# A constant row by selector matmuls, a first batch loaded by head group and a padded odd key chunk in a one-core attention and adapter-mixture kernel

## The chip, the cores and the metric

The kernel runs on one core of a Trainium2 chip. The metric is the device time of one execution, in microseconds (us), and smaller is better. A profile's span is some 1.7 us shorter than the time of the same execution (300.2 and 301.93 for the kernel before), so spans are compared with spans here and times with times.

Engines are named as in the profile: PE is TensorE's matmul, PEld its weight load, DVE is VectorE, ACT is ScalarE, POOL is GpSimd, SP is the engine that issues most of the DMAs. SPq is SP's time in issuing them.

On one core the "slow" state is only a label for runs over 1.5% above the fastest of the same kernel; ratios use the other runs, which the tables call fast. The one profile of the kernel before carries the slow label itself (301.93 us, clock 0.893), though it is only 0.5% above the fastest timed run of its call.

## The reference

Attention over 8 batches, 12 heads, 448 keys and 64 numbers per head, then a mixture of eight small adapters (rank 16), two of them chosen for each row:

```python
def _attn_ref(q, k, v):
    scores = np.matmul(q, k.transpose(0, 1, 3, 2)) / np.sqrt(64)
    attn = softmax(scores)                      # cut: the usual max, exp, sum
    return np.matmul(attn, v)                   # (8, 12, 448, 64)

def _moe_ref(x, w_gate, A, B):                  # x: (3584, 768)
    logits = x @ w_gate                         # 8 experts, the best two are kept
    # ... cut: w = softmax over the two
    delta = sum over the two of  w * ((x @ A[e]) @ B[e])
    return x + delta
```

## The kernel before

The kernel writes the attention output as a constant row plus a small rest. The constant row is the mean of v over the keys, one row of 768 numbers for a whole batch. The rest comes from exp(score) - 1 and from v less its mean, both in fp16. TensorE makes the means and keeps each as two fp16 halves, high and low, in a small tile `mhl` (called `s["m"]` in the code). For the adapters the constant row is multiplied once per batch by the weights (`cz`). That matmul contracts over the 768 numbers, so it needs the row turned upright: tile `mT`, with 128 partitions and six columns of chunks.

A list scheduler written in Python fixes, before anything runs, the order of the instructions on each engine. TensorE executes that order strictly: an instruction that waits stops all those behind it (from 90 to 103 us of the profile before, while one matmul waits, TensorE starts no other).

The constant row before (a scatter by eight DMAs, then a DMA transpose):

```python
def const_row(b):
    yM, mT = Buf(p_yM, "yM"), Buf(p_mT, "mT")
    for g in range(4):
        for j in range(2):
            P.op("SP", lambda e, g=g, h0=h0, j=j: [e.dma_start(        # L504
                V(yM)[32 * j:32 * j + 2, :]..., V(s["m"])[32 * g:32 * g + 2, :]...)],
                r=[s["m"], b_init], w=[part], holds=[yM], cost=0.06, dma=0.05, ...)
    P.op("SP", lambda e: [e.dma_start_transpose(V(mT)[:, :, 0:48], V(yM)[0:48, :])],   # L508
         r=parts + [yM, b_init], w=[mT], cost=0.06, dma=0.5, ...)
    def fc(e):
        for c in range(6):                                             # L515
            x = e.matmul(ps[:, V(tc), 0:144], V(mT)[:, c, :], W16[:, c, :], ...)
    # ... cut: two small vector instructions put the result into cz
```

The score tiles: each batch has 21 of them, each with one exp on ScalarE ("an exp" below is this instruction, 168 in all). They go in pairs through a ring of two PSUM slots of two banks each. `holds` of the first tile of a pair names both slots (the code is condensed):

```python
p_sc = Pool([(0, 1), (2, 3)])
...
prev = P.op("PE", fs, r=[g["qT"], g["kT"]], w=g["slot"],
            holds=[x for y in two[i:] for x in y["slot"]], ...)       # L473, L467
P.op("ACT", ... e.activation(E32, ps[slot], AF.Exp, scale=SC) ..., cost=0.80, tag="exp")   # L483
P.op("POOL", ... E16 = E32 * 1.0 - 1.0 ...)
```

The start of the program (condensed), which fixes what comes early:

```python
load_qk(0); load_v(0, q0[:2])
weights(v0)                      # w_gate, six pieces of A (L306), B
load_qk(1, v0); load_v(1, q0[-1:] + v0)
for b in range(NB):
    if b == 0:
        transposes(0, 0); transposes(0, 1); means(0); transposes(0, 2)
    for u in range(NU):          # three head groups of a batch
        attention(b, u, ...)
        if u == 0: const_row(b)
        if b + 1 < NB: transposes(b + 1, u)
    if b + 1 < NB: means(b + 1)
    if b >= 1: moe(b - 1)
```

The softmax here doesn't subtract the row's maximum and nothing guards it: scores larger than these inputs give would overflow.

Of the kernel before, what the change touches and what calls it, by code (L numbers as in the profile page):

```python
# [6 lines left out]
ALU = mybir.AluOpType  # L7
# [8 lines left out]
MO = 6.0  # L16
TO = -3.0
SO = -3.0
BI = 0.0
# [29 lines left out]
class Prog:  # L49
# [38 lines left out]
    def schedule(self, window=400):  # L88
# [4 lines left out]
        dmaq = {e: 0.0 for e in ENG}  # L93
        left = len(self.ops)
        LAT = 0.08

        def ready(o):
            t = 0.0
            e_pe = o.eng == "PE"
            for d in o.deps:  # L100
                if d.end is None:
                    return None
                t = max(t, d.end + (0 if d.eng == o.eng and d.dma is None and (e_pe or d not in o.raw) else LAT))
# [4 lines left out]
            for bs in need.values():  # L108
# [4 lines left out]
                for s in range(p.n):  # L113
                    ten = p.tenant[s]
                    if ten is None:
                        av.append(0.0)
                    elif ten.left == 0:
                        av.append(max(x.end for x in ten.ops) + LAT)
# [6 lines left out]
        while left:  # L125
# [43 lines left out]
            if o.dma is not None:  # L169
                free[e] = st + o.cost  # L170
                dmaq[e] = max(dmaq[e], st + o.cost) + o.dma
                o.end = dmaq[e] + 1.8
# [14 lines left out]
def bass_mha_softmax__then__mixture_of_adapters_kernel(  # L187
# [9 lines left out]
    with contextlib.ExitStack() as ctx:  # L197
# [15 lines left out]
        p_kT = pool("kT", 4, [128, 2, NS], F16)  # L213
# [7 lines left out]
        p_yM = pool("yM", 1, [48, ND], F16)  # L221
        p_mT = pool("mT", 1, [128, 6, 128], F16)
# [10 lines left out]
        sel2 = sb("sel2", [128, 128], F16)  # L233
        cS = sb("cS", [128, 3, 32])
# [13 lines left out]
        b_init = fixed("init")  # L248
# [12 lines left out]
        def setup_dve(e):  # L261
# [9 lines left out]
            for x in p_yM.views:  # L271
                i = e.memset(x[:, :], 0.0)
            for x in p_mT.views:
                i = e.memset(x[:, :, :], 0.0)
# [3 lines left out]
        def setup_dve2(e):  # L278
# [8 lines left out]
            for x in p_w16.views:  # L287
                xv = x.rearrange("p (h two) d -> p h two d", two=2)
                e.memset(xv[0:64, :, 0, 64:65], 1.0)
                i = e.memset(xv[64:128, :, 1, 64:65], 1.0)  # L290
# [8 lines left out]


        def weights(gate=()):
            P.op("SP", lambda e: [e.dma_start(wg32[:, :, :], moe_w_gate.rearrange("(c p) e -> p c e", p=128))],
                 w=[b_wg], cost=0.06, dma=1.0, prio=0.5, after=gate)
            bs = [fixed("A%d" % c) for c in range(6)]
            for c in range(6):
# [3 lines left out]
                    w=[bs[c]], cost=0.06, dma=1.2, prio=0.5, after=gate)  # L309
            P.op("SP", lambda e: [e.dma_start(B32[:, :], moe_B.rearrange("e r d -> (e r) d"))],  # L310
                 w=[b_B32], cost=0.06, dma=1.0, prio=0.5, after=gate)
# [10 lines left out]
        def load_qk(b, gate=()):  # L322
            s = st[b]
            pr = 6.0 * b - 9
            s["q"], s["k"] = Buf(p_q16, "q"), Buf(p_k16, "k")
            s["qp"] = {}
            groups = [(0, 2), (2, 6)] if b == 0 else [(0, 6)]
            for (h0, h1) in groups:
                for nm, src in (("q", q), ("k", k)):
                    for half in range(2):  # L330
                        part = fixed("ld")
                        for hs in range(h0, h1):
                            s["qp"][(nm, hs, half)] = part

                        def f(e, h0=h0, h1=h1, nm=nm, src=src, half=half):
                            dst = s[nm].pool.views[s[nm].slot]
                            return [e.dma_start(
                                dst[64 * half:64 * half + 64, h0:h1, :, :].rearrange("p h c d -> p h (c d)"),
                                src[b, 6 * half + h0:6 * half + h1, :, :].rearrange("h (p c) d -> p h (c d)", c=7))]
                        P.op("POOL", f, w=[part], holds=[s[nm]], cost=0.68, dma=0.32 * (h1 - h0), prio=pr, tag="ld", after=gate)  # L340

        def load_v(b, gate=()):
            s = st[b]
            pr = 6.0 * b - 8
            s["v"], s["w"] = Buf(p_v32, "v"), Buf(p_w32, "w")
            s["vp"] = []
            vv = v[b].rearrange("h (p c) d -> p h c d", c=7)
            for half in range(2):
                part = fixed("ldv")
                s["vp"].append(part)  # L350
                P.op("SP", lambda e, half=half: [e.dma_start(  # L351
                    s["v"].pool.views[s["v"].slot][64 * half:64 * half + 64, :, :, :].rearrange("p h c d -> p h (c d)"),
                    vv[:, :, 3 * half:3 * half + 3, :].rearrange("p h c d -> p h (c d)"))],
                    w=[part], holds=[s["v"]], cost=0.06, dma=2.0, prio=pr, after=gate, tag="ldv")
            for half in range(2):
                part = fixed("ldw")
                s["vp"].append(part)
                P.op("SP", lambda e, half=half: [e.dma_start(  # L358
                    s["w"].pool.views[s["w"].slot][64 * half:64 * half + 64, :, :],
                    v[b].rearrange("(h two) (p c) d -> two p h c d", c=7, two=2)[half, :, :, 6, :])],  # L360
                    w=[part], holds=[s["w"]], cost=0.06, dma=0.6, prio=pr, after=gate, tag="ldw")
# [4 lines left out]
        def transposes(b, u):  # L366
            s = st[b]
            pr = 6.0 * b + 2 * u + TO
            for nm, pl in (("q", p_qT), ("k", p_kT)):
# [4 lines left out]
                parts = [s["qp"][(nm, 2 * u, hf)] for hf in range(2)]  # L374
                order = list(range(7)) if nm == "q" else [0, 3, 1, 4, 2, 5, 6]
# [7 lines left out]
                P.op("PE", f, r=[src, b_id] + parts, w=[tb], holds=[dst], cost=0.42, prio=pr, mode="t", tag="tr", nsig=2)  # L383

                def ev(e, tb=tb, dst=dst, nm=nm):
                    bk = ps[:, V(tb), :].bitcast(F16)[:, 0:896].rearrange("p (c g x) -> p g c x", c=7, g=2)
# [303 lines left out]
        for b in range(NB):  # L690
# [8 lines left out]
            for u in range(NU):  # L699
                attention(b, u, last=(b == NB - 1 and u == NU - 1))  # L700
                if u == 0:
                    const_row(b)
# [154 lines left out]
```

## Time and profile before

| | kernel before |
|---|---|
| time, median of 3 | 300.35 us |
| span of the profile | 300.2 us |
| TensorE busy, idle | 217.4 us, 82.8 us (300.2 less 217.4) |
| exp number 21 ends (batch 0) | 52.6 us |
| exp number 42 ends (batch 1) | 109.3 us |
| exp number 168 ends (batch 7) | 269.9 us |

The ends of exps are read from ScalarE's timeline. They cut the span into stage 1 (batches 0 and 1), stage 2 (batches 2 to 7) and a tail (the last expert work).

From the first part of the page of the kernel before: busy time, share of the span and count of instructions.

```profile
span 300.2 us, 8596 instructions
PE 217.4 (72%) x3624; PEld 141.1 (47%) x3624; DVE 165.0 (55%) x461; ACT 169.4 (56%) x205; POOL 178.1 (59%) x211
```

No engine is full. The stretches view of the same kernel has for each stretch its length, then each engine's busy time with its count, then the granted TensorE clock, the DMA share and GB/s. These are the three stages:

```profile
0.00:109.30 109.30, 59.19 (x884) 36.60 (x885) 37.16 (x107) 46.78 (x54) 53.79 (x72) 0.78 0.87 144
109.30:269.90 160.60, 139.16 (x2514) 92.17 (x2510) 109.59 (x302) 120.62 (x148) 122.77 (x139) 0.98 0.78 133
269.90:300.20 30.30, 19.06 (x239) 12.38 (x235) 18.20 (x54) 2.01 (x5) 1.55 (x2) 0.84 0.42 112
```

Stage 1 takes 109.3 us for two batches, TensorE idles 50.1 us of it, and the clock is only 0.78. Stage 2 takes 160.6 us for six. The list of waits says what stage 1 waits for (waiter, releaser: us in total, times, longest):

```profile
PE ps L515 <- DMA mT<-yM: 26.7, 3, 13.6
ACT E_5 L483 <- PE ps L473: 26.1, 13, 7.5
ACT E_2 L483 <- PE ps L473: 22.2, 10, 14.4
```

The constant-row matmul waits 26.7 us, in three waits, for the transposed row. ScalarE's longest waits, 7.5 and 14.4 us, are the same stalls seen one engine further on. SP's timeline shows the path of that row (start, length, what):

```profile
18.84 11.08 SPq L306 DMA_DIRECT2D A<-in_moe_A_dram  x6
...
39.44 5.52 SPq L504 DMA_DIRECT2D yM<-mhl  x8
...
49.64 2.39 SPq L508 DMA_TRANSPOSE mT<-yM  x1
59.48 5.41 SPq L504 DMA_DIRECT2D yM<-mhl  x8
68.28 1.20 SPq L508 DMA_TRANSPOSE mT<-yM  x1
...
80.63 5.59 SPq L504 DMA_DIRECT2D yM<-mhl  x8
...
89.67 3.20 SPq L508 DMA_TRANSPOSE mT<-yM  x1
```

Eight issues cost SP about 5.5 us per batch, and the transpose can only be issued after them. The chain that ended last (start, length, what) shows how long its data then took to land:

```profile
49.64 9.76 DMA mT<-yM
...
68.28 2.43 DMA mT<-yM
...
89.67 13.44 DMA mT<-yM
```

All three lie on the critical chain, and they span 9.8, 2.4 and 13.4 us.

### The profile page before, as it was taken

How to read it: one execution, taken by the hardware profiler on the slowest of the kernel's cores; microseconds unless marked ns; L12 is line 12 of the kernel's file. 1: busy time of each engine (PE TensorE's matmuls, PEld its weight loads, DVE VectorE, ACT ScalarE, POOL GpSimd, SP SyncE). 2: the span in 40 equal slices, each digit the busy share in tenths (PEclk: the TensorE clock that was granted, in tenths of full speed). 3: DMA queues.
4: the chain of work that ended last, by engine and by line, in shares of the span. 5: the costliest groups of instructions: out<-in, count | busy, mean ns of one | idle time of the engine just before them, and what ended most of it. 6: DMA issues, size and time to landing. Idle time of an engine off the chain costs nothing.

```text
span 300.2 us, 8596 instructions
## 1 busy us (share of the span) xinstructions
PE 217.4 (72%) x3624; PEld 141.1 (47%) x3624; DVE 165.0 (55%) x461; ACT 169.4 (56%) x205; POOL 178.1 (59%) x211
## 2 busy tenths in 40 slices
PE   1757666075880286899979898898689988996863
PEld 0434434033560154466546655565356655765441
DVE  6116524040830136866677668666284787686664
ACT  1526385141780077787878786986269777870100
POOL 8258466241673068777989986797267867771000
PEclk9967959665996599999999999999699999999887
DMA  6979999836929703596994999299947233853326
GB/s 78 222 112 179 189 229 212 143 48 125 176 69 210 102 4 48 115 272 99 164 173 87 242 123 211 68 244 137 140 130 149 56 88 63 110 133 82 99 84 183
DMA packets 68966, 40.54 MB, mean 135 GB/s; under 512 B 40640, under 2 KB 65216, under 8 KB 68928
## 3 DMA queue, kind: packets, MB, share of 16 engines
q1 hardware_dynamic: 56064, 28.99, 50.7%
q0 software_dynamic: 12864, 11.01, 26.2%
q8 instruction: 28, 0.46, 0.7%
q14 instruction: 10, 0.08, 0.1%
HBM read 33.84 MB, written 11.01 MB: 149 GB/s over the span
## 4 chain that ended last, share of the span: by engine, by line
PE 35%; DMA 15%; SPq 14%; ACT 13%; DVE 12%; issue 6%; POOL 4%; DVEq 0%; POOLq 0%; ACTq 0%
DMA mT<-yM 9%; PE ps L548 8%; PE ps L473 6%; SPq L504 5%; DMA v_0<-in_v_dram 4%; PE ps L660 4%; SPq L306 4%; SPq L358 4%; PE ps L407 3%; PE ps L664 3%; ACT E_1 L483 2%; PE ps L550 2%; ACT E_0 L483 2%; SPq L351 2%; PE ps L467 2%
## 5 line engine op out<-in xcount | busy, mean ns | idle before, releaser
L473 PE MATMUL ps<-qT,kT 64*128 64x448 f16 x288 | 45.3, 378 | 15.3 <-ACT E_1 L483 5.5
L483 ACT ACTIVATE E_5<-ps 128x896 f32<-128x896 f32 x28 | 25.7, 918 | 26.1 <-PE ps L473 26.1
L483 ACT ACTIVATE E_2<-ps 128x896 f32<-128x896 f32 x28 | 25.8, 922 | 22.3 <-PE ps L473 22.2
L388 ACT COPY kT<-ps 128x896 f16<-128x896 f16 x24 | 21.9, 912 | 16.6 <-PE ps L380 16.6
L483 ACT ACTIVATE E_4<-ps 128x896 f32<-128x896 f32 x28 | 25.7, 918 | 9.8 <-PE ps L473 9.7
L483 ACT ACTIVATE E_1<-ps 128x896 f32<-128x896 f32 x28 | 25.7, 917 | 8.6 <-PE ps L473 8.5
L483 ACT ACTIVATE E_0<-ps 128x896 f32<-128x896 f32 x28 | 25.7, 916 | 8.1 <-PE ps L473 8.1
L483 ACT ACTIVATE E_3<-ps 128x896 f32<-128x896 f32 x28 | 25.8, 921 | 5.8 <-PE ps L473 5.8
L660 PE MATMUL ps<-B,zT 128*128 128x384 f16 x64 | 22.6, 353 | 4.7 <-DVE qT L388 1.4
L515 PE MATMUL ps<-W,mT 128*128 128x144 f16 x48 | 5.4, 261 | 27.2 <-DMA mT<-yM 26.7
L556 DVE TENSOR_SCALAR den<-ps 128x8 f32<-128x8 f32 x48 | 7.9, 165 | 30.5 <-PE ps L550 30.3
L388 DVE COPY qT<-ps 128x896 f16<-128x896 f16 x24 | 14.9, 620 | 17.0 <-PE ps L380 16.8
L473 PEld LDWEIGHTS ps<-qT,kT 64*128 64x128 f16 x288 | 9.5, 95 | 29.0 <-issue 6.6
L664 PE MATMUL ps<-mhl,sel 128*128 128x192 f16 x128 | 22.5, 261 | 0.0
L518 DVE CAST cz<-ps 64x144 f16<-64x144 f32 x8 | 2.4, 298 | 28.5 <-PE ps L515 28.5
L515 PEld LDWEIGHTS ps<-W,mT 128*128 128x128 f16 x48 | 3.8, 111 | 28.7 <-issue 14.3
L417 DVE CAST mhl<-ps 128x192 f16<-128x192 f32 x8 | 2.9, 357 | 23.6 <-PE ps L411 23.6
L664 PEld LDWEIGHTS ps<-mhl,sel 128*128 128x128 f16 x128 | 13.2, 103 | 4.9 <-issue 1.2
L467 PE MATMUL ps<-qT,kT 64*64 64x448 f16 x96 | 15.4, 404 | 0.0
L635 PE MATMUL ps<-W,yT 128*128 128x128 f16 x192 | 14.2, 219 | 0.0
L660 PEld LDWEIGHTS ps<-B,zT 128*128 128x128 f16 x64 | 6.3, 98 | 16.7 <-issue 2.2
L486 POOL TENSOR_SCALAR E_6<-E_3 128x896 f16<-128x896 f32 x5 | 4.7, 937 | 15.0 <-ACT E_3 L483 15.0
(276 smaller groups left out, 852.3 us busy)
## 6 DMA issues: line engine op xcount, KB each, us to landing
v_0<-in_v_dram SPq DMA_DIRECT2D x8, 576.0 KB
v_1<-in_v_dram SPq DMA_DIRECT2D x8, 576.0 KB
q_1<-in_q_dram POOLq DMA_DIRECT2D x8, 336.0 KB, 6.4
k_1<-in_k_dram POOLq DMA_DIRECT2D x8, 336.0 KB, 8.3
out_dram<-o_0 SPq DMA_DIRECT2D x13, 192.0 KB
out_dram<-o_1 SPq DMA_DIRECT2D x12, 192.0 KB, 3.0
out_dram<-o_4 SPq DMA_DIRECT2D x11, 192.0 KB, 3.3
q_0<-in_q_dram POOLq DMA_DIRECT2D x6, 336.0 KB, 9.1
```

Of the source, the lines that this page charges most:

```text
L306: P.op("SP", lambda e, c=c: [e.dma_start(A32[:, c, :].rearrange("p (e r) -> p e r", e=NE), moe_A[:, 128 * c:128 * c + 128, :].rearrange("e ...
L358: P.op("SP", lambda e, half=half: [e.dma_start(s["w"].pool.views[s["w"].slot][64 * half:64 * half + 64, :, :], v[b].rearrange("(h two) (p ...
L388: return [e.tensor_copy(o, bk) if nm == "q" else e.copy(o, bk)]
L467: r.append(e.matmul(ps[sl, bk, 0:NS], V(kT)[sl, pi, 384:448], V(qT)[sl, pi, :], start=True, stop=True, tile_position=(64 * h, 64 * h)))
L473: r.append(e.matmul(ps[:, bk, 0:NS], V(kT)[sl, pi, 128 * t:128 * t + 128], V(qT)[sl, pi, :], start=True, stop=True, tile_position=(64 * h, ...
L483: P.op("ACT", lambda e, g=g, e32=e32: [e.activation(V(e32)[:, :, :], ps[:, V(g["slot"][0])[0]:V(g["slot"][0])[0] + 2, 0:NS], AF.Exp, scale ...
L504: P.op("SP", lambda e, g=g, h0=h0, j=j: [e.dma_start(V(yM)[32 * j:32 * j + 2, :].rearrange("p (h x) -> p h x", h=12)[:, h0:h0 + 5:2, :], V ...
L515: x = e.matmul(ps[:, V(tc), 0:144], V(mT)[:, c, :], W16[:, c, :], start=(c == 0), stop=(c == 5))
L548: e.matmul(o, V(gs[c])[:, hi, c0:c0 + 128], V(s["v16"])[:, h, c, :], start=(c == 0), stop=False)
L635: e.matmul(o, V(yT[t])[:, c, :], W16[:, c, 0:128], start=(c == 0), stop=False)
L660: e.matmul(ps[:, V(to), 0:384], V(zT)[:, t, :], B16[:, 384 * hh:384 * hh + 384], start=True, stop=True, skip_group_check=True)
L664: x = e.matmul(ov[:, par, :, :], sel[:, 2 * par + hh, :], V(m)[:, :], start=False, stop=True, skip_group_check=True)
```

## The change

Its intent is to take the constant row off the DMA queue, to let the first batch start on a third of its data, and to give the odd key chunk (keys 384 to 447 of two head pairs) the same matmul form as the full chunks. The scheduler's costs and priorities were retuned at the same time. The core of the diff, with cuts:

```diff
-TO = -3.0
-SO = -3.0
+TO = -2.5
+SO = -1
-        LAT = 0.08
+        LAT = {"PE": 0.2, "ACT": 0.18, "DVE": 0.12, "POOL": 0.12, "SP": 0.1}
-        dmaq = {e: 0.0 for e in ENG}
+        dmaq = 0.0
...                                            (and many cost= and dma= figures)
-            for g in range(4):                            # constant row: 8 DMAs
-                for j in range(2):
-                    P.op("SP", ... e.dma_start(V(yM)[32 * j:32 * j + 2, :]..., V(s["m"])[32 * g:...]))
-            P.op("SP", lambda e: [e.dma_start_transpose(V(mT)[:, :, 0:48], V(yM)[0:48, :])], ...)
+            def fm(e):                                    # 6 selector matmuls
+                for par in range(2):
+                    for j in range(3):
+                        i = e.matmul(ps[64 * par:64 * par + 64, V(tm), 68 * j:68 * j + 68],
+                                     V(s["m"])[:, 64 * j:64 * j + 64], selT[:, par, :, :]...,
+                                     start=True, stop=True, tile_position=(0, 64 * par))
+            P.op("PE", fm, ...)
+            P.op("DVE", ... e.tensor_copy(V(mT)..., ps[:, V(tm), 0:204]...) ...)
...
-                order = list(range(7)) if nm == "q" else [0, 3, 1, 4, 2, 5, 6]
+                order = list(range(7)) if nm == "q" else [6, 0, 3, 1, 4, 2, 5, 6]
...                                            (odd chunk: 128 wide, two matmuls into one bank)
-                                    r.append(e.matmul(ps[sl, bk, 0:NS], V(kT)[sl, pi, 384:448], V(qT)[sl, pi, :],
-                                                      start=True, stop=True, tile_position=(64 * h, 64 * h)))
+                                    kc = V(kT)[sl, 896:1024] if pi == 0 else V(kT)[sl, 0:128]
+                                    r.append(e.matmul(ps[:, bk, 0:NS], kc, V(qT)[sl, pi, :], start=(pi == 0), stop=(pi == 1),
+                                                      tile_position=(64 * h, 0)))
...
-        load_qk(0)
-        load_v(0, q0[:2])
-        weights(v0)
-        load_qk(1, v0)
-        load_v(1, q0[-1:] + v0)
+        for u in range(NU):
+            load_qk(0, (u,))
+        load_v(0, (0,), q0[:2])
+        load_v(0, (1, 2), q0[:2])
+        load_qk(1, gate=v0)
+        load_v(1, gate=v0)
+        weights(v0)
...
-                transposes(0, 1)
-                means(0)
-                transposes(0, 2)
+                means(0, (0,))
             for u in range(NU):
                 attention(b, u, last=(b == NB - 1 and u == NU - 1))
+                if b == 0 and u < 2:
+                    transposes(0, u + 1)
+                    if u == 0:
+                        means(0, (1, 2))
                 if b + 1 < NB:
                     transposes(b + 1, u)
```

## The prediction

> **What bounds it now.** Busy table: TensorE 217.4 of 300.2 us (72%), no other engine above 59%. The stretches view splits the span: 104.5 to 271.5 us is a steady part with TensorE 145 of 167 us busy at clock 0.97, bounded by TensorE plus short score-exp round trips; 271.5 to 300 is a serial tail (last expert stage); 0 to 104.5 holds only two of the eight batches and is bounded by waits. TensorE executes in order, and the list of waits names them: constant-row matmul <- DMA mT, 26.7 us in 3 waits, the longest 13.6. They lie at 54-60, 66-71 and 90-103 us. The SP timeline shows why: eight scatter issues of 0.62 to 0.7 us each per batch (64 = 42 us of queue in all), then a DMA transpose which lands after 2.4, 9.8 and 13.4 us because bulk loads are in flight. The clock there is 0.60 to 0.63. Also: 3.2 us until v of batch 0 lands (18.8), 5 us at 35-40 for ScalarE's cast of B (its DMA sits behind 11 us of A issues), and 3.8 us at 209 without a releaser.
>
> **Removed.** The scatter, the transpose, and with them all 26.7 us of wait, and most half-clock restarts (estimate 5 us, from those clocks). v of batch 1 is issued ahead of the weights (was 30.6 us, now about 18.5), so the 5 us ScalarE wait should go.
>
> **Added.** Six small matmuls and one vector copy per batch (estimate 0.3 and 0.35 us, from similar ones here); 48 more transposes, 0.036 us each from 0.5 us per 14: 1.7 us; two more vector subtractions per batch, vector being 67% busy in the steady part: nothing. The odd chunk keeps four 448-column matmuls (0.50 us a group, full chunks 0.48): nothing.
>
> **Moved.** The built order of TensorE puts q transposes and means of batch 1 before the third head group of batch 0. So after 14 exps (about 30 us) I expect TensorE to wait for v of batch 1. At the measured 172 GB/s (2.75 MB landed by 18.4 us) that lands at 34-36: a new wait of 4 to 8 us. Loading by head group itself gains 1 to 3 us: batch 1's loads still wait for batch 0's v. From about 38 us 28 exps at 1.2 us (the undisturbed pace at 76-89 us) put the end of batch 1's exps near 72 us, against 109. The y transposes now come amid loads, so the first expert stage may wait 0 to 5 us.
>
> **Sum.** 300.4 - 37 (first two batches) - 4 (order, part of the 3.8) = 259 us. 80%: 249 to 272. Faster by over 2%: 0.97; within 2%: 0.02; slower: 0.01.
>
> **Signs.** Right: no wait of the constant-row matmul above 1 us; exp number 42 ends at 66-80 us; the stretch from it to the last exp stays 155-168 us and the tail 27-30; mean clock rises from 0.89 to 0.93 or more; a wait of TensorE for v of batch 1 near 30-36 us. Wrong: a new multi-microsecond wait for yT, W or later loads in 50-110 us.
>
> **What could make it wrong.** The loads: 40.5 MB pass in 259 us at 156 GB/s, while the busiest stretches reached about 200; if loads fall behind, the steady pace slows (time up to 275). Or the steady part was itself limited by late buffers and gains from the retuned scheduler costs (down to 248). The Trainium skill ("TensorE: Matmul & The Clock Gate", What's actually happening) says idle windows of about 3.4 us halve the clock; this trace agrees (0.60 at 89.7-104.5), so every wait removed or added counts for more than its length.

## More of the kernel before

The time scatters more than usual for this kernel. The kernel before took 300.3 to 300.89 us on the first chip and 287 to 305 us in the five later calls.

Where few runs are fast, their mean is the mean of the luckiest, so the text also looks at the median of all.

## The result, and the profile after

The changed kernel took 275.56 us, the median of 4 runs (274.39 to 277.66), beside 300.5 us (300.3 to 300.89) for the kernel before. Its results are correct. The ratio is 0.9176, with a 95% interval of 0.9118 to 0.9234. (A ratio here is the mean time of one kernel's fast runs over that of the other's of the same rounds, so it is not quite the ratio of the medians.) It is faster, as predicted, but 16.6 us slower than the 259 us predicted and outside the range of 249 to 272.

| us | before | after | difference |
|---|---|---|---|
| span | 300.2 | 272.7 | -27.5 |
| TensorE busy | 217.4 | 212.2 | -5.2 |
| TensorE idle | 82.8 | 60.5 | -22.3 |
| exp 14 ends | 39.9 | 28.6 | -11.3 |
| exp 21 ends | 52.6 | 53.5 | +0.9 |
| exp 42 ends | 109.3 | 80.8 | -28.5 |
| exp 42 to exp 168 | 160.6 | 160.8 | +0.2 |
| tail | 30.3 | 31.1 | +0.8 |

The first part of the page of the changed kernel:

```profile
span 272.7 us, 8828 instructions
PE 212.2 (78%) x3756; PEld 142.1 (52%) x3756; DVE 170.1 (62%) x502; ACT 169.0 (62%) x205; POOL 180.4 (66%) x215
```

The stretches view of the changed kernel, with the same three stages and columns as before:

```profile
0.00:80.80 80.80, 52.31 (x883) 33.53 (x883) 37.54 (x127) 45.42 (x54) 54.21 (x74) 0.92 1.01 162
80.80:241.60 160.80, 141.53 (x2645) 96.65 (x2642) 113.73 (x321) 121.63 (x149) 125.08 (x141) 0.98 0.80 145
241.60:272.70 31.10, 18.37 (x241) 11.87 (x237) 18.88 (x55) 1.99 (x5) 1.14 (x2) 0.92 0.43 114
```

All of the gain lies in stage 1, and within it in batch 1: exps 22 to 42 took 27.3 us instead of 56.7. The clock of stage 1 rose from 0.78 to 0.92. Stage 2 did not move. The changed kernel's list of waits:

```profile
ACT E L515 <- PE ps L505: 50.8, 66, 1.9
...
ACT kT L403 <- PE ps L393: 18.3, 5, 9.8
```

The waits for the constant row's DMA are gone. ScalarE still waits 50.8 us in all for scores, but in 66 short waits, none above 1.9 us. A new wait of 9.8 us stands in the second line. Where it lies, ScalarE's timeline of the changed kernel shows (idle time before a piece and its releaser are in brackets):

```profile
26.83 1.73 ACT L515 ACTIVATE E<-ps 128x896 f32<-128x896 f32 x2 [0.49 <-PE ps L505]
38.36 2.57 ACT L403 COPY kT<-ps 128x896 f16<-128x896 f16 x3 [9.81 <-PE ps L393]
...
51.90 0.83 ACT L316 CAST W<-A 128x768 f16<-128x768 f32 x1 [4.39 <-DMA A<-in_moe_A_dram]
```

ScalarE finishes the 14th exp at 28.6 us and has nothing to do until 38.4. TensorE's timeline for those microseconds, same kernel:

```profile
31.05 1.58 PE L393 MATMUL ps<-ident,q 128*64 128x128 f16 x28
33.67 0.58 PE L393 MATMUL ps<-ident,q 128*64 128x128 f16 x14
35.17 1.18 PE L430 MATMUL ps<-v,cS 128*32 128x192 f32 x24 [0.92 <-DMA vr<-in_v_dram]
...
37.66 1.17 PE L393 MATMUL ps<-ident,k 128*64 128x128 f16 x32 [0.47 <-DVE mhl L441]
```

TensorE transposes q of batch 1 and makes the means of batch 1's v (L430), and only then transposes the k that the third head group of batch 0 needs. It waits for data only 0.92 us of that. The reason is in the code: the buffers for the transposed q and k are handed out strictly in the order in which the program creates them, and the changed start creates those of batch 1's first group before those of batch 0's third.

The second new wait, 4.39 us for A at 47.5 to 51.9 us, comes from SP's timeline of the changed kernel. The same six issues took 11.08 us before:

```profile
22.68 23.08 SPq L310 DMA_DIRECT2D A<-in_moe_A_dram  x6
```

They now run beside the loads of batch 1. As a result the constant-row matmul of batch 0 meets a wait after all, though not for its own data; from the list of TensorE's waits in that stretch:

```profile
PE ps L550 <- DVE W L320: 3.2, 1, 3.2
```

### The profile page after: what moved, and what is told of

It reads as the page before. It is cut to its first block, busy times and chain, and to the rows that moved or that the text cites. A ratio compares the mean times of both kernels' runs of the same rounds, so it can differ in the third digit from the quotient of the medians.

```text
span 272.7 us, 8828 instructions
## 1 busy us (share of the span) xinstructions
PE 212.2 (78%) x3756; PEld 142.1 (52%) x3756; DVE 170.1 (62%) x502; ACT 169.0 (62%) x205; POOL 180.4 (66%) x215
## 3 DMA queue, kind: packets, MB, share of 16 engines
q0 software_dynamic: 12928, 11.01, 27.3%
## 4 chain that ended last, share of the span: by engine, by line
PE 44%; DVE 19%; SPq 10%; DMA 8%; ACT 8%; POOL 6%; issue 3%; DVEq 0%; POOLq 0%
PE ps L583 12%; PE ps L505 8%; SPq L310 6%; ACT E L515 6%; DVE v L469 6%; POOL E L518 4%; DMA A<-in_moe_A_dram 4%; PE ps L695 4%; PE ps L393 3%; PE ps L585 3%; PE ps L430 3%; DVE o L703 3%; PE ps L670 3%; DVE y L599 3%; DVE vr L460 3%
## 5 line engine op out<-in xcount | busy, mean ns | idle before, releaser
L518 POOL TENSOR_SCALAR E<-E 128x896 f16<-128x896 f32 x168 | 154.2, 940 | 53.0 <-ACT E L515 50.5
L515 ACT ACTIVATE E<-ps 128x896 f32<-128x896 f32 x168 | 145.4, 918 | 51.0 <-PE ps L505 50.8
L583 PE MATMUL ps<-v,E 128*128 128x65 f16 x1152 | 59.3, 199 | 8.5 <-POOL E L518 3.6
L583 PEld LDWEIGHTS ps<-v,E 128*128 128x128 f16 x1152 | 52.8, 100 | 19.3 <-DVE y L599 4.7
L585 PE MATMUL ps<-vr,E 128*128 128x65 f16 x384 | 54.8, 196 | 0.0
L703 DVE SCALAR_TENSOR_TENSOR o<-y,ps 128x384 f32<-128x384 f16 x64 | 34.6, 550 | 10.2 <-PE ps L699 8.3
L585 PEld LDWEIGHTS ps<-vr,E 128*128 128x128 f16 x384 | 38.7, 101 | 0.0
L599 DVE TENSOR_TENSOR y<-ps,den 128x512 f16<-128x512 f32 x48 | 33.1, 689 | 1.0
L403 ACT COPY kT<-ps 128x896 f16<-128x896 f16 x24 | 21.8, 914 | 18.3 <-PE ps L393 18.3
L469 DVE TENSOR_TENSOR v<-v,ps 128x576 f16<-128x576 f32 (+1 forms) x32 | 22.1, 727 | 0.3
L699 PE MATMUL ps<-mhl,sel 128*128 128x192 f16 x128 | 21.8, 254 | 0.0
L393 PE MATMUL ps<-ident,k 128*64 128x128 f16 x384 | 16.2, 233 | 5.0 <-DVE v L469 2.4
L393 PEld LDWEIGHTS ps<-ident,q 128*64 128x64 f16 x336 | 11.3, 119 | 14.7 <-DMA q<-in_q_dram 6.9
```

What stands on the lines that cost most here:

```text
L393: x = [e.transpose(bk[64 * h:64 * h + 64, 128 * i:128 * i + 128], V(src)[:, 2 * u + h, c, :], ident[:, :]) for h in range(2)]
L403: return [e.tensor_copy(o, bk) if nm == "q" else e.copy(o, bk)]
L469: return [e.tensor_tensor(v16[:, f, h, :, :], v32[:, f, h, :, :], mb[:, f, :, None, :].broadcast_to([128, nu, 3, DH]), ALU.subtract)]
L515: P.op("ACT", lambda e, g=g, e32=e32: [e.activation(V(e32)[:, :, :], ps[:, V(g["slot"][0])[0]:V(g["slot"][0])[0] + 2, 0:NS], AF.Exp, scale ...
L518: P.op("POOL", lambda e, g=g, e32=e32: [e.tensor_scalar(V(g["e16"])[:, :, :], V(e32)[:, :, :], 1.0, -1.0, ALU.mult, ALU.add)], r=halves + ...
L583: e.matmul(o, V(gs[c])[:, hi, c0:c0 + 128], V(s["v16"])[:, h, c, :], start=(c == 0), stop=False)
```

## The experiments

Eighteen kernels ran, in five calls, each call on one chip. Two theories stand at the start. Theory one: stage 1 fell short of the prediction because of named, mendable waits there (the order of batch 0's third group; the A loads), and mending them brings the missing time back. Its rival: those waits are in the shadow of something else, and the missing time went elsewhere, into stage 2 or into the nature of the steady part.

| kernel | chip's call | median, us (range) | fast mean, us (runs) | ratio to before |
|---|---|---|---|---|
| constant row alone | 1 | 271.54 (268.67-273.52) | 270.58 (3 of 4) | 0.9204 |
| third group first | 1 | 269.29 (268.32-270.70) | 269.40 (4 of 4) | 0.9164 |
| A in long rows | 1 | 272.14 (270.00-273.91) | 272.05 (4 of 4) | 0.9277 |
| old priorities | 1 | 275.68 (273.56-276.31) | 275.31 (4 of 4) | 0.9365 |
| the change | 2 | 272.09 (270.27-277.17) | 271.82 (5 of 6) | - |
| third first + cost of A | 2 | 275.74 (271.71-280.22) | 273.17 (3 of 6) | - |
| old scheduler | 2 | 280.62 (273.35-282.35) | 274.78 (2 of 6) | - |
| old odd chunk | 2 | 273.30 (271.75-276.33) | 272.83 (5 of 6) | - |
| the change | 3 | 275.07 (270.34-277.48) | 271.07 (2 of 6) | 0.9231 |
| third first + weights early | 3 | 270.22 (268.02-274.99) | 269.75 (5 of 6) | 0.9186 |
| constant row alone, again | 3 | 268.61 (266.80-270.44) | 268.65 (6 of 6) | 0.9161 |
| third first + old odd chunk | 3 | 272.51 (267.09-278.81) | 268.38 (2 of 6) | 0.9139 |
| the change | 4 | 275.83 (274.94-280.15) | 275.84 (5 of 6) | - |
| + TensorE work | 4 | 277.78 (274.66-279.19) | 276.57 (4 of 6) | - |
| + VectorE work | 4 | 275.73 (274.06-278.93) | 275.38 (5 of 6) | - |
| constant row, weight casts later | 4 | 268.93 (267.36-270.31) | 269.02 (6 of 6) | - |
| constant row + own slot only | 5 | 257.53 (255.47-259.07) | 257.34 (6 of 6) | 0.8806 |
| the change + own slot only | 5 | 272.48 (265.49-274.70) | 265.61 (2 of 6) | 0.9101 |

In the calls without a ratio, the kernel before had too few fast runs for one. For calls 3 and 5, where 4 and 3 of its 11 runs were fast, the record gives the ratios but leaves each verdict "unclear"; for call 1 it says "faster". Where a stage is quoted below it comes from the one profile of that kernel.

### 1. The constant row alone

The kernel before with nothing but the constant row's hunk (which also gives `mT` two buffers in place of one and narrows it; these were not separated), once in call 1 and once more, unaltered, beside the change in call 3.

```diff
 (kernel before)
-            yM, mT = Buf(p_yM, "yM"), Buf(p_mT, "mT")        # 8 DMAs + DMA transpose
+            tm, mT = Buf(p_t, "tm"), Buf(p_mT, "mT")         # 6 matmuls + 1 copy
             ... (as in the change, nothing else)
```

> The kernel before with the constant row alone changed (selector matmuls and a vector copy for the 8 scatters and the DMA transpose); loads, odd chunk and scheduler constants as before. If the constant row is nearly all of the gain: the holes at 53-60, 66-72 and 90-103 us close, exp 42 ends at 78 to 85 us, time 268 to 278. If the head-group loading, odd chunk and retuned constants carry a good part: time 283 to 292, with exp 42 after 90 us.

> The constant row alone in the kernel before, again, now beside the control. If it carries the whole gain: ratio to the control 0.99 to 1.01. If loads, odd chunk and retuning add to it: 1.015 or more; if they cost: 0.985 or less. Second stage 156 to 159 us, first stage 83 to 85.

Measured: 270.58 us for the fast runs in call 1, and 268.65 in call 3, where the whole change had 271.07 (2 fast runs) and a median of 275.07. Its ratios to before are 0.9204 and 0.9161, beside 0.9176 and 0.9231 for the whole change. By the medians of call 3 it is 6.5 us under the whole change (268.61 and 275.07). So the constant row alone gives the whole gain, as far as this scatter lets one see. The stretches view of the constant row alone (call 3):

```profile
0.00:80.00 80.00, 54.01 (x905) 34.45 (x906) 37.05 (x111) 46.62 (x54) 53.41 (x72) 0.89 1.09 183
80.00:234.50 154.50, 138.22 (x2542) 91.35 (x2538) 110.79 (x307) 120.65 (x147) 123.25 (x139) 1.00 0.77 142
```

Stage 1 is as long as in the change (80.0 and 80.8). Stage 2 is shorter, 154.5 us, and 157.2 in the other profile of it (a run labelled slow), where the four profiles of the whole change have 160.8, 162.4, 163.6 (labelled slow) and 164.4. Between fast profiles that is 154.5 against 160.8 to 164.4, and with a further edit that leaves its later stages alone (experiment 8) it is 156.1. In stage 2 the change has some 100 more matmuls (2645 and 2542) and 3.0 us more of idle TensorE. In the ledger of TensorE the constant row alone takes 29.0 us from the idle time (82.8 to 53.8) and 6.1 from the busy time (217.4 to 211.3), with 48 more matmuls, so the latter is probably the clock (0.78 to 0.89 in stage 1). Nothing that the rest of the change adds can be seen.

### 2. The third head group of batch 0 first

```diff
 (changed kernel)
-                if b == 0 and u < 2:
-                    transposes(0, u + 1)
-                    if u == 0:
-                        means(0, (1, 2))
+                if b == 0 and u == 0:
+                    transposes(0, 1)
+                    means(0, (1, 2))
+                    transposes(0, 2)
```

> The changed kernel, but the transposes of batch 0's third head group are created before those of batch 1's first one, so they come out ahead of them in the first-in first-out order of the transposed-q and -k buffers. Theory order: ScalarE's 9.8 us gap at 28.6-38.4 us is TensorE doing batch 1's work first, so the gap falls under 4 us, and exp 42 ends 4 to 7 us earlier, time 268 to 272. Rival, data: batch 1's loads set the pace of the first 80 us anyway, so the gap moves behind batch 0's 21 exps and exp 42 ends within 2 us of 80.9, time 273 to 277.

The edit did in stage 1 what theory one says. From ScalarE's timeline of this kernel, the gap of 9.81 us has become one of 2.83, and exp 21 ends at 39.5 us instead of 53.5:

```profile
33.25 1.73 ACT L515 ACTIVATE E<-ps 128x896 f32<-128x896 f32 x2 [0.56 <-PE ps L505]
37.80 0.91 ACT L403 COPY kT<-ps 128x896 f16<-128x896 f16 x1 [2.83 <-PE ps L393]
```

The stretches view of the same kernel:

```profile
0.00:71.40 71.40, 47.58 (x892) 31.12 (x892) 37.62 (x127) 46.00 (x54) 55.44 (x76) 0.95 1.10 181
71.40:237.00 165.60, 142.32 (x2630) 96.78 (x2630) 113.82 (x322) 120.67 (x147) 123.58 (x139) 0.98 0.82 142
```

Exp 42 now ends at 71.4 us, the 72 of the prediction, but stage 2 has become 165.6 us, longer than in any of the four profiles of the change. The fast runs average 269.40 us. In its call the nearest thing to the unaltered change is experiment 4, at 275.31, so the edit may be worth some 6 us there; with a second edit it was worth nothing in the next call (experiment 5), and beside early weights 1.3 us (experiment 6). The medians of experiment 6 would give the pair of edits 4.9 us. A few microseconds at most, and not the 16.6 that were missing.

### 3. A in long rows

The six loads of A move pieces of 64 bytes (16 numbers of 4 bytes, by the code). Here they read rows of 512 bytes from v instead. The result is wrong (relative error 0.15), which was expected.

```diff
 (changed kernel)
-                    A32[:, c, :].rearrange("p (e r) -> p e r", e=NE),
-                    moe_A[:, 128 * c:128 * c + 128, :].rearrange("e p r -> p e r"))],
+                    A32[:, c, :],
+                    v[0, c].rearrange("(p c) d -> p (c d)", c=2)[0:128, :])],
```

> Wrong result on purpose: the six A loads keep their bytes, place and order, but read 512 contiguous bytes per partition (from v) and not 8 pieces of 64 bytes. Theory collision: the A issues shrink from 23 us to about 4-5 us, ScalarE's 4.4 us wait for A and TensorE's 3.2 us behind it vanish, batch 0's 21 exps end about 4 us earlier, time 269 to 273. Rival: loads of batch 1 and 2 are bound by bytes, so something else is waited for, time 273.5 to 277.

The wait of ScalarE for A is gone, and SP's issues of A take 11.34 us instead of 23.08. Exp 42 ends at 77.6 us, and in the second profile of the unaltered change it ends at 77.8. The time, 272.05 us, lies in theory one's range and 3.3 us under experiment 4 of the same call, but also inside the change's scatter (271.82 in the next call). So the A loads cost the whole 3 us at most, and this run does not decide between theory and rival. ScalarE's gap before exp 15 was 11.54 us in this kernel, so the third group's gap stayed and even grew.

### 4. The old priorities

```diff
 (changed kernel)
-TO = -2.5
-SO = -1
+TO = -3.0
+SO = -3.0
```

> The changed kernel with the two priority constants of before (transposes -3, means -3 in place of -2.5 and -1); scheduler costs as changed. Theory late means: means come later with -1 and the centering of v lands on the chain; then the steady batches 3 to 7 (27.1 us mean) return to 25.5 to 26.3 and time is 268 to 273. Rival added work, or the new scheduler costs: batches stay at 26.8 to 27.4 and time within 2 us of 275.6.

Measured 275.31 us, with stages of 77.1, 163.5 and 31.2 us. That is the change within its scatter. The two priorities are worth nothing that can be seen.

### 5. Third group first and an honest cost of A; the old scheduler; the old odd chunk

The unaltered change ran again with these three, on one chip.

> The changed kernel once more, unedited, as the control of this call (kernels of different calls may sit on chips that differ by 2%). Ratio to before 0.915 to 0.925; about 45 us of gap structure as before: exp 21 ends at 51 to 54 us, exp 42 at 78 to 81 us, batches 3 to 7 at 26.5 to 27.5 us each.

The change took 271.82 us (fast runs), with stages of 77.8, 162.4 and 31.0.

The first of the three tells the scheduler what an A load costs when it is slow:

```diff
 (changed kernel, with the edit of experiment 2, and)
-                    w=[bs[c]], cost=2.2, dma=0.9, prio=0.5, after=gate)
+                    w=[bs[c]], cost=3.85, dma=1.6, prio=0.5, after=gate)
```

> Third head group first, as in the second experiment, and the scheduler told that an A issue takes 3.85 us (the 23.1 us measured, over six), so that ScalarE's cast of W stands later in its order. Theory: ScalarE's 4.8 us wait for A and TensorE's 4.0 us behind it vanish on top of the 9.8 us gap; exp 42 ends at 66 to 69 us (71.4 with the order alone), ratio to the control 0.955 to 0.97. Rival: the casts' place does not matter since batch 1 is bound by its loads: exp 42 at 71 to 73, ratio 0.975 to 0.985.

Exp 42 ends at 69.0 us, the earliest so far, and the kernel is not faster: 273.17 us, 1.0050 times the change of its call, a ratio outside both expected ranges. Stage 2 has grown to 169.8 us, 9.0 more than in the first profile of the change. Its clock is 0.95 there, beside 0.95 to 0.98 in the profiles of the change, and 21.8 us of it are idle. The stretches view of this kernel, around a place where the clock drops:

```profile
162.00:165.00 3.00, 1.37 (x20) 0.66 (x22) 2.96 (x6) 2.23 (x3) 2.54 (x4) 0.89 0.00 0
165.00:171.00 6.00, 6.00 (x92) 4.23 (x89) 3.31 (x14) 3.41 (x4) 4.87 (x6) 0.50 1.00 190
```

TensorE was busy 1.37 of 3 us, in short gaps, and then ran 6 us at half clock. The unaltered change of the same call has nearly the same low stretch without the drop:

```profile
162.00:165.00 3.00, 1.58 (x30) 0.73 (x24) 2.52 (x5) 2.94 (x5) 1.82 (x3) 1.00 0.00 0
165.00:168.00 3.00, 2.14 (x59) 1.68 (x60) 2.31 (x6) 2.12 (x3) 3.00 (x5) 1.00 0.46 88
```

None of the gaps here is longer than about 1.3 us, and the clock is still halved. Whether a given stretch is hit differs from run to run, which is a likely part of the scatter; that part is argued, not measured.

The second of the three has all scheduling constants of the kernel before (priorities, latencies, costs, one model DMA queue per engine) in the changed kernel:

```diff
 (changed kernel)
-        LAT = {"PE": 0.2, "ACT": 0.18, "DVE": 0.12, "POOL": 0.12, "SP": 0.1}
+        LAT = 0.08
-        dmaq = 0.0
+        dmaq = {e: 0.0 for e in ENG}
 ...                         (and TO, SO, all cost= and dma= figures as before)
```

> The changed kernel with all scheduler costs, latencies and priorities of before (the instructions are the same, only their order differs). Theory retuning costs the steady part: batches 2 to 7 sum to 155 to 158 us as in the constant-row-only kernel (156.6), against 160.3. Rival added work: they stay at 159 to 164. The first two batches may move either way, so the verdict is the sum of the batches, not the time.

Only two of six runs were fast (274.78), so its time is not used; the profile was a slow run. Its stages are 88.3, 161.3 and 31.0 us. Even in this slow run stage 2 is not longer than in the change, so the steady part gives no sign of noticing the old constants; more than a hint this is not.

The third has the odd key chunk, its 14 transposes and its order of vr as before:

```diff
 (changed kernel)
-                order = list(range(7)) if nm == "q" else [6, 0, 3, 1, 4, 2, 5, 6]
+                order = list(range(7)) if nm == "q" else [0, 3, 1, 4, 2, 5, 6]
-                                    r.append(e.matmul(ps[:, bk, 0:NS], kc, V(qT)[sl, pi, :], start=(pi == 0), ...
+                                    r.append(e.matmul(ps[sl, bk, 0:NS], V(kT)[sl, pi, 384:448], V(qT)[sl, pi, :], ...
```

> The changed kernel with the odd chunk as before (14 transposes of k and 64-wide weights, centering of the odd rows in two operations per batch); constant row, loads and scheduler as changed. Theory odd chunk costs: batches 2 to 7 sum 155 to 158 us and time 2 to 4 us under the control. Rival it is neutral: 159 to 162 and time within 1.5 us of the control. If the padded chunk helps (no switch of tile shape): 162 to 165.

Measured 272.83 us, 1.0 more than the change of its call, with stages of 77.0, 161.9 and 31.1. The odd chunk's new form is neutral.

### 6. Weights early; third group first with the old odd chunk

> Control: the changed kernel unedited, in one call with the next three so that their ratios to it do not depend on the chip. Median 270 to 276 us; up to exp 42: 77 to 82 us; from there to the last exp 160 to 163 us; tail 31.

The change in this call: median 275.07, stages of 80.2, 163.6 and 31.1.

```diff
 (changed kernel, with the edit of experiment 2 and A's cost of 3.85, and)
-        weights(v0)                 # after batch 1's loads
+        weights(q0[:2])             # ahead of them, prio -7.5
```

> Third head group first, and the weights issued right after batch 0's v and ahead of batch 1's v (no wait for v of batch 0), with the casts late in ScalarE's order. Theory: no wait for W (it has landed by 35 us), v of batch 1 lands later, but by 42 us, so exp 42 ends at 64 to 69 us and the total is 0.965 to 0.98 of the control. Rival, found in the last call: TensorE is the bound and exp 42 coming earlier leaves more of its other work undone, so the second stage grows to 165 to 170 us, and the ratio is 0.985 to 1.0.

Exp 42 ends at 63.9 us, 16.9 earlier than in the change and below the prediction's 66 to 80. The time is 269.75 us. The stretches view of this kernel shows why:

```profile
0.00:63.90 63.90, 41.33 (x684) 25.08 (x684) 27.03 (x101) 45.93 (x54) 52.59 (x72) 0.95 1.14 182
63.90:237.30 173.40, 153.84 (x2838) 106.76 (x2838) 123.88 (x348) 121.02 (x147) 126.95 (x142) 0.95 0.79 143
```

By exp 42 TensorE has done 684 matmuls, where the change had done 883. The exps were let ahead of other work, and that work was done later: stage 2 has 2838 matmuls instead of 2645. The early marker was borrowed from the later stage. This is what theory one cannot see, and it is why exp 42 is no measure of progress. It does not explain experiments 2 and 5: there 892 and 860 matmuls were done by exp 42, nearly as many as in the change, and TensorE then idled 23.3 and 21.8 us of stage 2, where it idles 19.3 in the change. Why, stays open.

> Third head group first, with the odd chunk as before. Theory: first stage 70 to 73 us from the order, second 160 to 163 us: total 0.97 to 0.98 of the control. If the order's gain is given back by a lower clock or displaced TensorE work, as with the late casts: second stage 166 or more and ratio 0.985 to 1.0.

The edit of experiment 2 with the odd chunk of `old odd chunk` gave 268.38 us (two fast runs, median 272.51), with stages of 76.4, 160.4 and 31.1: by the fast means 2.7 us less than the change, by the medians 2.6, again within the scatter.

### 7. More TensorE work, more VectorE work

If stage 2 is bound by the amount of TensorE's work, more of it must lengthen it. One kernel does the q transposes of batches 2 to 6 twice: 210 more, 7.5 us by an estimate from 0.5 us per 14 in the profile before. The other does the copies of the same q tiles twice, 15 copies of 0.62 us, or 9.3 us of VectorE.

```diff
 (changed kernel: TensorE)
-                    for i, c in enumerate(order):
+                    for i, c in list(enumerate(order)) * (2 if 2 <= b < 7 and nm == "q" else 1):
 (changed kernel: VectorE)
+                    if nm == "q" and 2 <= b < 7:
+                        e.tensor_copy(junk[:, 3 * (b - 2) + u, :].rearrange("p (g c x) -> p g c x", g=2, c=7), bk)
```

> Control of this call: the changed kernel unedited. 270 to 277 us; first stage 77 to 82 us, second 160 to 164, tail 31.

> The changed kernel with the 14 transposes of q done twice (same values) for batches 2 to 6: 15 groups of 0.50 us, so 7.5 us more on TensorE and nothing else; order unchanged. Theory TensorE bounds the stretch after exp 42: that stretch grows by 6 to 8 us and so does the time. Rival round trips: TensorE's idle time takes it up, growth under 3 us.

> The changed kernel with the copy of transposed q out of PSUM done twice on the vector engine for batches 2 to 6: 15 copies of 0.62 us, 9.3 us more on the vector engine; order unchanged. Theory TensorE bounds: growth under 3.5 us. Rival, the vector engine is on the chain nearly always: growth of 6 to 9 us.

Stage 2 in the stretches view, for the change of this call:

```profile
79.60:244.00 164.40, 144.93 (x2644) 99.15 (x2641) 113.84 (x321) 121.72 (x148) 125.05 (x141) 0.95 0.76 141
```

With more TensorE work:

```profile
79.30:242.70 163.40, 145.81 (x2813) 101.02 (x2810) 114.14 (x321) 122.06 (x149) 125.09 (x141) 0.98 0.78 142
```

With more VectorE work:

```profile
81.00:242.60 161.60, 141.96 (x2653) 96.94 (x2650) 119.86 (x333) 121.86 (x149) 125.18 (x141) 0.98 0.76 144
```

The extra work is there (169 more matmuls, 6.0 us more VectorE time in this stage) and costs 0.7 us and -0.5 us in the fast means. Neither amount bounds stage 2. One reserve: the clock was 0.95 in the profile of the plain change and 0.98 in the others, so the busy times of TensorE are not compared. What is the same in every row, of every kernel, is the 120.6 to 122.1 us of ScalarE; the rest of the stage is ScalarE's gaps.

### 8. The weight casts moved away

In the constant row alone, ScalarE waits 3.2 and 1.9 us for A and B at the casts of the weights (near 32 and 36 us), with exps behind them. Here the casts and batch 0's constant row come after exp 21.

```diff
 (constant row alone)
+        def casts(bs):
+            last = [o for o in P.ops if o.tag == "exp"][20]
+            P.op("ACT", lambda e: [e.copy(W16[:, :, 0:128], A32[:, :, :])], ..., after=[last])
+            P.op("ACT", lambda e: [e.copy(B16[:, :], B32[:, :])], ..., after=[last])
```

> The constant row alone, and ScalarE's two weight casts placed after batch 0's last exp, as a dependency, so that no exp waits behind them for A. If that wait (7.8 us in the first such run) is on the chain: exp 21 ends 4 to 8 us earlier (43 to 48) and the time is 262 to 267 us, 2 to 5 under the kernel without it. If it is in the shadow of something else, as with the contiguous A: within 1.5 us of 268.6.

Measured 269.02 us, beside 268.65 for the constant row alone in the call before. ScalarE did pass the casts freely, and then waited 7.77 us for TensorE at 41 us; TensorE itself waited 5.11 us, until 45.8, for vr of batch 1. The cast's wait had been lying in the shadow of those loads. Another named wait taken away for nothing.

### 9. Each score tile waits for its own slot only

What remains is the ring of scores. From ScalarE's timeline in the steady part of the constant row alone:

```profile
125.76 1.73 ACT L485 ACTIVATE E<-ps 128x896 f32<-128x896 f32 x2 [1.13 <-PE ps L475]
127.97 1.73 ACT L485 ACTIVATE E<-ps 128x896 f32<-128x896 f32 x2 [0.49 <-PE ps L475]
130.42 1.73 ACT L485 ACTIVATE E<-ps 128x896 f32<-128x896 f32 x2 [0.72 <-PE ps L475]
```

Two exps, a gap, two exps, and so on through the whole stage: 53 gaps in stage 2, which sum to 33.8 us; 24 of them are of 0.48 to 0.50 us. The Trainium skill ("Perfetto Trace Analysis", Optimization Strategy) says that a gap which repeats on the engine that should be full can mean too few buffers in PSUM. The trace agrees in form. In the code the first tile of a pair waits for both slots, so TensorE begins a new pair only when both exps are done. The edit is one line. The scheduler plans with that line too, so the order of all instructions changes with it:

```diff
 (constant row alone; and the same line in the changed kernel)
-                    prev = P.op("PE", fs, r=[g["qT"], g["kT"]], w=g["slot"], holds=[x for y in two[i:] for x in y["slot"]],
+                    prev = P.op("PE", fs, r=[g["qT"], g["kT"]], w=g["slot"], holds=g["slot"],
```

> The constant row alone (268.6 us at best so far), and a score tile waits for its own PSUM slot only, not for both of its pair. Theory ring (ScalarE 122 us plus 52 gaps of 0.49 us and more): most of the 0.49 us gaps close, the stretch after exp 42 falls from 154-157 to 138-150 us, time 253 to 264. Rival: TensorE, which executes in order, is then late in other places (its tiles change shape more often), and the stretch falls by less than 3 us or grows: 266 to 272.

Measured 257.34 us, all six runs fast, correct. The ratio to before is 0.8806 (0.8741 to 0.887), where the constant row alone has 0.9161 and the change 0.9176. It beats both kernels: its slowest run, 259.07, lies below the fastest of any other kernel here. Yet the stage after exp 42 did what the rival said. ScalarE's timeline in the steady part of this kernel:

```profile
122.43 3.34 ACT L485 ACTIVATE E<-ps 128x896 f32<-128x896 f32 x4 [0.34 <-PE ps L475]
...
163.46 3.35 ACT L485 ACTIVATE E<-ps 128x896 f32<-128x896 f32 x4 [1.43 <-PE ps L475]
168.39 2.54 ACT L485 ACTIVATE E<-ps 128x896 f32<-128x896 f32 x3 [1.58 <-PE ps L475]
```

Exps run up to four in a row. The gaps of 0.49 us are nearly all gone (3 instead of 24), but 16 are now longer than 1.4 us, where there were 2. In sum ScalarE's gaps in stage 2 did not shrink: 34 of them, 34.8 us. The stretches view of this kernel:

```profile
0.00:69.20 69.20, 49.99 (x760) 30.48 (x760) 33.26 (x102) 44.41 (x53) 48.42 (x65) 0.90 1.04 167
69.20:225.80 156.60, 147.12 (x2653) 98.92 (x2654) 113.73 (x314) 121.15 (x150) 126.94 (x145) 1.00 0.89 158
```

So the gain did not come in the steady part, for which the edit was meant, and the hit on the time is in part luck. Over the whole span ScalarE's waits for scores did fall, from 49.8 to 41.4 us, but mostly in stage 1. Stage 2 is no shorter than in the constant row alone (156.6 and 154.5). It holds 111 more matmuls, left over from stage 1, and has 9.5 us of TensorE idle time instead of 16.3. Stage 1 is 10.8 us shorter. The ledger of the whole span is the safer account: TensorE's idle time fell from 53.8 to 39.8 us, while its busy time grew from 211.3 to 217.4, which gives 7.9 us of span. (The times differ by more, since these two profiles are the slowest run of the one and the fastest of the other.) From the two pages, constant row alone first:

```profile
PE 211.3 (80%) x3672; PEld 137.9 (52%) x3672; DVE 166.2 (63%) x470; ACT 169.2 (64%) x205; POOL 178.1 (67%) x211
PE 217.4 (85%) x3672; PEld 142.4 (55%) x3672; DVE 166.7 (65%) x470; ACT 167.5 (65%) x205; POOL 177.2 (69%) x211
```

TensorE's waits for an exp before a score tile fell only from 7.5 to 5.1 us. Its idle time before the matmuls of the attention weights with v fell from 8.9 to 0.4, and before one group of expert matmuls (L640) from 3.7 to 0.3. That the line gives the gain is shown; whether by the freed slots or by the new order that comes with it is not.

> The changed kernel with the same edit. Theory ring: the stretch after exp 42 falls from 161-164 to 145-157 us, time 262 to 271. Rival: it falls by less than 3 us, time 272 to 278.

In the whole change the same line gave two fast runs at 265.61 us and four slow ones up to 274.70; the profile is one of the slow ones, so no stage of it is used as evidence. The ratio of 0.9101 is better than the change's, and much worse than 0.8806.

## Why the prediction was right and wrong, point by point

Right:

- The direction (faster by more than 2%) and the cause of the gain. The constant row's DMA path held TensorE up, its 26.7 us of waits are gone, and by experiment 1 this hunk alone is worth the whole gain.
- "Most half-clock restarts (estimate 5 us)", in sign. TensorE's busy time fell by 5.2 us with 132 more matmuls, and by 6.1 with the constant row alone. But the four profiles of the unaltered change have 212.2, 212.2, 216.1 and 217.4 us of it, so against the 217.4 before the fall is anything from none to 5.2.
- "The odd chunk ... nothing". Restoring it moved the time by 1.0 us, within the scatter.
- "Loading by head group itself gains 1 to 3 us." Stage 1 is 77.8 to 80.8 us in the change and 80.0 to 83.7 with the constant row alone. That fits, but no run isolates the loading, and stage 2 gave it back.
- The signs on the clock (0.95, "0.93 or more"; the four runs of the result have 0.91 to 0.95) and on the length of stage 2 (160.8, "155-168").

Wrong. In spans, the prediction wanted a fall of 41.4 us (300.35 less 259) and the profile shows 27.5, so 13.9 are missing. Stage 1 accounts for 8.8 of them, stage 2 for 4.2 and the tail for the remaining 0.9. (In times the miss is 16.6 us, because the profile before is a run 1.6 us above its median and the one after a run 1.2 us below.)

- "From about 38 us 28 exps at 1.2 us (the undisturbed pace at 76-89 us) put the end of batch 1's exps near 72 us." This is the main step that failed. The exps took up again at 40.8 us and ended at 80.8, so 40.0 us for 28, or 1.43 us each: 6.4 us from the pace and 2.8 from the start (against the 71.6 that the prediction's figures give). What broke the pace is mostly the wait for A of 4.39 us, which the prediction counted as gone. Two more profiles of the change have waits for A of 4.2 and 4.7 us and 1.42 and 1.40 us for an exp; the fourth has a wait of 1.7 us and a pace of 1.26, and experiment 3, without the wait, 1.29. In stage 2 of the change an exp takes 1.28 us (160.8 over 126).
- The step behind it, that an earlier exp 42 shortens the whole by as much. Experiments 2, 5 and 6 reached 71.4, 69.0 and 63.9 us, as early as predicted or earlier, and the kernels stayed near 270. For the last of them the matmul counts show the work pushed into stage 2; for the other two it is open where the gain went. The prediction's own list of single terms came to less: 26.7 for the waits, 5 for the clock, 5 for the cast, 2 for the head groups, less 6 for v and 2 for added work is 30.7, and 300.35 less 30.7 is 269.7, inside the range. The marker's 37 was taken instead, and 4 more added.
- "TensorE to wait for v of batch 1 ... a new wait of 4 to 8 us." The size and the place of the gap were nearly right (9.8 us of ScalarE at 28.6 to 38.4), but only 0.9 us of it is TensorE's wait for v. It is the order, made by handing out buffers first come, first served. It can be mended without any faster load, as experiment 2 shows.
- "V of batch 1 is issued ahead of the weights, so the 5 us ScalarE wait should go." It was exchanged for one of 4.4 us for A, since the A issues, now beside batch 1's loads, took 23.1 us. It mattered less for the whole than for the pace of stage 1: experiment 8 took such waits away and gained nothing, and experiment 3 gained 3 us at most.
- "Constant-row matmul above 1 us: none." It waits 3.2 us, once, for the weights.
- "- 4 (order, part of the 3.8)" from the retuned scheduler. The runs give nothing: old priorities and old costs leave stage 2 where it was (163.5, and 161.3 in a slow run). Stage 2 did fall by 3.4 to 6.1 us with the constant row alone, and in the whole change nothing of that is left.
- "Bounded by TensorE plus short score-exp round trips." The first half fails as far as the amount of work goes: experiment 7 finds room on TensorE for 7.5 us of it. The second half is not shown. Experiment 9 changes the rule of the round trips with one line and gains about 11 us (268.65 to 257.34, on two chips; by the ratios to before, 3.9%), but in the steady part, of which the sentence speaks, ScalarE's gaps keep their sum.

What stays open:

- Which part of the change makes its stage 2 some 6 us longer than that of the constant row alone. The odd chunk, the priorities and the costs, undone one at a time, do not bring it back; their combinations and the new order of the first loads were not tried.
- By which way the line of experiment 9 gains: the freed slots, or the new order of all instructions.
- Why the change with own slots only has two levels, 265.5 and 272 to 275 us.
- A hole of 3.8 us on TensorE at 209 us in the kernel before, for which the profile names no releaser. The prediction counted on part of it; no experiment touched it.

## What to carry to other kernels

A tiny rearrangement of data that an in-order engine waits for is worth moving from the DMA queue to that engine: six small matmuls and a copy replaced nine DMAs and removed 23 to 29 us (medians of calls 1 and 3), and nothing else in a large change was needed for it. When you price a change, add the idle and busy time of the bounding engine over the whole span, and don't read a gain from a progress marker such as "the 42nd exp", which moves as soon as the order of work does. Where the engine that should be full shows the same short gap again and again, look at what the refill waits for: letting each tile wait for its own buffer gave about 11 us on the constant row alone, where all the retuning gave nothing that can be seen. Then check where the gain came from, since here the gaps kept their sum.

## What the Trainium skill lacked or had wrong

- "TensorE: Matmul & The Clock Gate", What's actually happening: it gives idle windows of about 3.4 us as what halves the clock. Here TensorE busy 1.37 of 3 us, in several short gaps, was followed by 6 us at 0.50, and a like stretch (1.58 and then 2.14 of 3 us) was not. The page's section "A second HAM failure mode: psum-queue depth-cycling" does describe a clock that swings because of brief idling between groups of matmuls, and this case agrees with it; it gives no busy share at which that threatens, and the first of these stretches lie near half (0.46 and 0.53 of 3 us); what decides between them is not shown.
- "DMA: Bandwidth & Descriptors", Issuing engines are not separate DMA queues: it says that the sequencer's time to initiate a DMA is usually small relative to the DMA. Here six issues of a tile in 64-byte pieces held SP's queue 23.1 us in the changed kernel, or 3.8 each beside a median of 11.1 us from issue to landing, with 187 GB/s in flight. They took 11.1 us in the kernel before, at 152 GB/s, and 11.3 in the changed kernel with rows of 512 bytes, at 213 GB/s. What is behind them on the queue waits as long.
- "DMA: Bandwidth & Descriptors", DMA Transpose (X-bar): that section lists constraints, and no time from issue to landing for a small transpose. From issue to landing a transpose of 48 rows of 768 took 2.4, 9.8 and 13.4 us here, with 31, 175 and 181 GB/s of DMA traffic in those stretches. The six selector matmuls that replace it take about 0.2 us each and overlap (192 to 265 ns in the trace, 0.29 us for all six where nothing is in the way).
- "Perfetto Trace Analysis", Optimization Strategy: it speaks of too few buffers as the cause of repeating gaps. Here the number of PSUM slots stayed at two, and only the rule by which a tile waits for them was changed, with the order that follows from it: gaps of 0.48 to 0.50 us on ScalarE in stage 2 went from 24 to 3, but their sum with the others stayed (33.8 and 34.8 us). That the hold can be wider than the need, and that the regular gap can give way to fewer long ones, would be worth a line.
